# Retention and a mixture of experts in one kernel: the rows of zeros are written one per expert, and the fill branches are read by two engines alone

## The chip, the cores and the metric

One core of a Trainium2 chip runs the whole program. The metric is the device time of one execution in microseconds. The kernel before was timed in three runs: 432.47, 430.78 and 431.31 us, median 431.31. A separate execution was profiled; the rows and lines below come from it.

Engines: PE is TensorE (PEld its weight loads), DVE is VectorE, ACT is ScalarE, POOL is GpSimd, SP is SyncE, which issues most DMAs. POOL issues the indirect DMAs, those whose target rows are given by a list of indices.

## The reference

Two parts follow each other. The first is linear attention with a decay per head ("retention"); the second sends each of the 3072 tokens through the one of 8 experts that its gate likes best. Both in float32:

```python
# q, k, v: (4, 8, 768, 64)
for t in range(S):
    state = gamma[None, :, None, None] * state + np.einsum('bhd,bhe->bhde', k[:, :, t], v[:, :, t])
    y[:, :, t] = scale * np.einsum('bhd,bhde->bhe', q[:, :, t], state)
x = y.transpose(0, 2, 1, 3).reshape(3072, 512)

e_idx = np.argmax(x @ w_gate, axis=1)            # gate_w: softmax probability of e_idx
eom = 1.0 / (1.0 + np.exp(-(x @ w_output_gate)))
for e in range(8):
    mask = e_idx == e
    h = np.maximum(x[mask] @ w1[e], 0.0)         # (n, 512) @ (512, 1024)
    out[mask] = gate_w[mask, None] * eom[mask, e, None] * (h @ w2[e])
```

## The kernel before

**Attention loop.** The tokens are taken in 12 pairs of 128-row chunks. Pass j of the loop `for j in range(1, NPR - 1)` (L714 to L769) does the scores of pair j (`w`, L356), the output from the state (`py <- qt, sd`, L373) and from the scores (`py <- am, vs`, L380), and for pair j-1 the gate's logits, the choice of the expert, a place in the expert's stretch, and an indirect DMA that scatters the token's row to that place in a DRAM buffer `srt` (`scatter`, L532). `srt` has 448 slots for each expert. The instructions of every engine run in the order in which the code is written.

**Rows that stay empty.** An expert gets fewer than 448 tokens, so the slots behind its count hold nothing of this execution. They must say "no token" before they are read. `pad` (L186) writes rows of zeros to the slots from 320 on that are behind the count (indices of filled slots are out of bounds and skipped). If an expert has so few tokens that slots below 320 are empty too, `fill` (L543) does the rest, in branches: once for the first expert (L734, on the number `late`), and once for all (L831 and L835, on `n_low`). Such a branch needs the number in a register of each engine, which `nc.values_load` reads (TENSOR_LOAD), and a compare-and-branch.

**Experts.** The expert that leads after the first passes is taken first, in two halves: 224 rows are loaded in the attention loop (`head_load`, L580) and computed between the last attention passes (`head_all`, generator steps pulled by `run_head`), the rest is "expert 0" of the main loop. Then the seven others follow in the order of their counts. The main loop (L1042 on) has steps s, eight (f = 0 to 7) for each expert e: `stage1(s)` is h = x w1 for 128 columns (L899, 12 matmuls) with a relu on ACT and a low part on DVE, `stage2(s - 2)` adds to the output (L917, 12 matmuls). Every operand is split into a high and a low part, so three matmuls stand for one. At f = 1 SP issues the load of the next expert's rows (`load_x`, L848), which DVE and ACT turn and split in the steps that follow (L876, L877, L883). The output rows of expert e - 1 are sent on POOL, two DMAs a step (`emit`); those of the first half, seven, one a step while e = 0 (`emit_head`, L1072).

**Where the zeros are written.** `new_pad` (L975) issues the next `pad` on POOL behind a given instruction. Three are written in the code between the attention and the main loop (behind the relu of head steps 5, 6 and 7), the other four at steps 2 to 5 of the main loop behind that step's `stage2`. The tracker of dependencies sees one buffer `srt`, so each `new_pad` waits for earlier loads of `srt`, except those listed in `x0`, which holds the load of expert 0 alone.

Of the kernel before, what the change touches and what calls it, by code (L numbers as in the profile page):

```python
# [26 lines left out]
SEG = 130  # L27
ROW = 4 * SEG
NOID = float(1 << 20)


@with_exitstack
def retention_moe_kernel(
# [14 lines left out]
    nc = tc.nc  # L48
    P = 128
    B, H, S, D = q.shape  # L50
    E, DM, DF = w1.shape
# [7 lines left out]
    NF = DF // P  # L59
# [27 lines left out]
    n_low = cpool.tile([P, 2], I32, name="n_low")  # L87
    late = cpool.tile([P, 1], I32, name="late")
# [36 lines left out]
    def last_consts():  # L125
        nc.gpsimd.memset(zrow, 0.0)
        nc.gpsimd.memset(zrow.rearrange("p (a x) -> p a x", x=SEG)[:, :, P:P + 1], NOID)
        nc.gpsimd.memset(capk, float(SLOTS))
# [40 lines left out]
    def low_weights(s: int):  # L169
        subs.pop(s)()  # L170
# [31 lines left out]
    with tc.manual_schedule(engines=None), ExitStack() as actx:  # L202
# [27 lines left out]
        def load_pair(j):  # L230
            if j > 4:
                load_q(j)
                load2(vn, v, "vn", j, 2)
                load2(kn, k, "kn", j, 3)
            else:
                load2(kn, k, "kn", j, 3)
                load_q(j)
                load2(vn, v, "vn", j, 2)
# [55 lines left out]
        def prep_q(j, engine, after=()):  # L294
            qr[j] = ap.tile([P, 2, H, D], F32, name="qr", tag="qr", bufs=1)
            t = qn.pop(j)
            for r in range(2):
                o = engine.tensor_copy(qr[j][:, r], t[:, :, r])
                if r == 0:
                    behind(o, after)  # L300
# [242 lines left out]
        def fill(base, cnt, lo, hi, pool):  # L543

            for j in range(lo, hi, P):
# [6 lines left out]

                nc.vector.tensor_scalar(out=fi, in0=cnt, scalar1=sf, scalar2=NOID, op0=ALU.is_gt, op1=ALU.mult)
                ii = pool.tile([P, 1], I32, name="ii", tag="ii")
# [23 lines left out]
        hd = {}  # L578
# [93 lines left out]
        def read_pick():  # L672
            rank_e[0] = nc.values_load(pick[0:1, 0:1], engines=(mybir.EngineType.SP,), min_val=0, max_val=E - 1)
# [6 lines left out]
        def judge():  # L680
            first_count()
            nc.vector.tensor_scalar(out=late, in0=cnt0, scalar1=float(HEAD), scalar2=None, op0=ALU.is_lt)
            fi = sm.tile([P, 1], F32, name="fi0", tag="fi0")
            nc.vector.tensor_scalar(out=fi, in0=cnt0, scalar1=slot, scalar2=NOID, op0=ALU.is_gt, op1=ALU.mult)
            nc.vector.scalar_tensor_tensor(out=pad0, in0=slot, scalar=base0, in1=fi, op0=ALU.add, op1=ALU.add)
# [28 lines left out]
        for j in range(1, NPR - 1):  # L714
            if j + 2 < NPR:
                load_pair(j + 2)
            if j - 1 == PICK + 1:
                read_pick()
            if j in w_at:
                load_weights(w_at[j])  # L720
            if j - 2 == EARLY:
                scatter(j - 2, 0)
                scatter(j - 2, 1)
            prep_q(j + 1, nc.gpsimd, [rt["done"]] if j >= 2 else ())
            prep_v(j + 1, nc.gpsimd)
            if j >= 2 and j - 2 != EARLY:
                scatter(j - 2, 0)
            open_y()
            scores(j, (lambda: state(1, 0)) if j == 1 else None)
            if j - 1 in w_at:  # L730
                cast_weights(w_at[j - 1])
            inter(j)
            if j == EARLY + 2:
                n_late = nc.values_load(late[0:1, 0:1], min_val=0, max_val=1)  # L734
                with tc.If(n_late > 0):
                    fill(base0, cnt0, 0, HEAD, sm)
                head_load()
                load_weights(4)
            logits(j - 1)
            turn_k(j + 1)  # L740
            turn_l(j - 1)
            route1(j - 1)
            exps(j - 1)
            attend(j, 0)
            weigh(j, 0)
            if j % NJ < NJ - 1:
                state(j, 1)
            turn_q(j + 1)
            gates(j - 1)
            for c in {1: (3, 4), 2: (5,)}.get(j, ()):  # L750
                more_gq(c, nc.vector)
            if j - 1 in w_at:
                low_weights(w_at[j - 1])
            if j - 2 == PICK:
                choose()
            tokens(j - 1)
            labels(j - 1)
            rows(j - 1)
            counts(j - 1)
            if j >= 2 and j - 2 != EARLY:  # L760
                scatter(j - 2, 1)
            places(j - 1)
            if j - 1 == PICK:
                sort8(cnts, io8, pick)
            if j - 1 == EARLY:
                judge()
            attend(j, 1)
            weigh(j, 1)
            state(j + 1, 0)  # L769
# [58 lines left out]
        cast_weights(6)  # L828
        run_head(12)
        low_weights(6)  # L830
        n_few = nc.values_load(n_low[0:1, 0:1], min_val=0, max_val=E)  # L831
        with tc.If(n_few > 0):
            for e in range(E):
                fill(float(e * SLOTS), cnts[:, e:e + 1], FILL - P, FILL, sm)
            n_few = nc.values_load(n_low[0:1, 1:2], min_val=0, max_val=E)  # L835
            with tc.If(n_few > 0):
                for e in range(E):
                    fill(float(e * SLOTS), cnts[:, e:e + 1], 0, FILL - P, sm)

    with tc.manual_schedule(engines=None), ExitStack() as mctx:  # L840
# [7 lines left out]
        def load_x(e):  # L848
            r0, n = PASS[e]
            nb = math.ceil(n / 32)  # L850
            t = mp.tile([P, NB, SEG], F32, name="xl", tag="xl")
            for a in range(4):
                ld = nc.sync.dma_start(
                    t[32 * a:32 * a + 32, 0:nb],
                    srt[ds(r0, 32 * nb), a * SEG:(a + 1) * SEG].rearrange("(n i) x -> i n x", i=32))
                if e == 0:
                    behind(ld, sent)
                    x0.append(ld.ins)
                else:
                    behind(ld, pads[e:e + 1])  # L860
                    for o in pads[:e] + pads[e + 1:]:
                        tc.declare_no_dep(ld.ins, o, reason="other experts' rows")
            xr[e] = t

        def turn_x(e, dc):
# [101 lines left out]
        def prep_idl(m):  # L967
            t = mp.tile([P, NTB], I32, name="idl", tag="idl", bufs=1)
            nc.vector.tensor_scalar(out=t, in0=m, scalar1=0.25, scalar2=None, op0=ALU.mult)
            return t  # L970

        x0 = []
        pads = list(hd["pad"])

        def new_pad(after):  # L975
            r = len(pads)
            o = pad(padr[:, r - 1:r])
            behind(o, [after])
            for ld in x0:
                tc.declare_no_dep(o.ins, ld, reason="other experts' rows")  # L980
            pads.append(o.ins)

# [21 lines left out]
        fj = rpool.tile([P, E], F32, name="fj")  # L1004
        nc.vector.tensor_scalar(out=fj, in0=ck, scalar1=slot, scalar2=NOID, op0=ALU.is_gt, op1=ALU.mult)
        nc.vector.scalar_tensor_tensor(out=fj, in0=ordf, scalar=float(SLOTS), in1=fj, op0=ALU.mult, op1=ALU.add)
        nc.vector.tensor_scalar(out=padr, in0=fj, scalar1=slot, scalar2=None, op0=ALU.add)
        new_pad(hd["relu", 5])
        run_head(24)
        new_pad(hd["relu", 6])  # L1010
        run_head(12)
        turn_x(0, 0)
        turn_x(0, 1)
# [28 lines left out]
        for s in range(NS + 2):  # L1042
            e, f = divmod(s, NF)
            while loaded < min(NS, s + NF + 1):
                load_weights(loaded)
                loaded += 1
            if f == 1 and e + 1 < E:
                load_x(e + 1)
            if s == NS - NF:
                idm = load_idl(E - 1)  # L1050
            if s < NS:
                relu = stage1(s)
            if s >= 2:
                done = stage2(s - 2)
                if s - 2 < NF and len(pads) < E:
                    new_pad(done)
                if f == 1:
                    copy_out(s - 2)
            if e == 0:
                for n in SPLIT.get(f, ()):  # L1060
                    split_weights(n)
                for dc in {4: (0,), 5: (1,), 6: (2, 3)}.get(f, ()):
                    prep_x(1, dc)
            else:
                if 3 <= f < 7 and e + 1 < E:
                    prep_x(e + 1, f - 3)
                for n in SPLIT.get(s, (s + NF - 2,)):
                    if n < NS:
                        split_weights(n)
            if s == NS - NF + 3:  # L1070
                idl = prep_idl(idm)
            if e == 0:  # L1072
                if f < HEAD // 32:
                    behind(emit_head(f), [relu])
            elif s < NS and f >= 1:
                for n in range(2 * f - 2, min(math.ceil(PASS[e - 1][1] / 32), 2 * f)):
                    behind(emit(e - 1, n), [done if n % 2 else relu])
# [5 lines left out]
    with tc.If(odd > 0):  # L1083
        with ExitStack() as octx:
# [72 lines left out]
            for r in range(1, E):  # L1157
                nov = nc.values_load(over[0:1, r - 1:r], min_val=0, max_val=SLOTS)
                with tc.If(nov > 0):
                    e = nc.values_load(order[0:1, r - 1:r], engines=(mybir.EngineType.SP,), min_val=0, max_val=E - 1)  # L1160
# [47 lines left out]
```

## Time and profile before

| | |
|---|---|
| median of three runs | 431.31 us (430.78 to 432.47) |
| the profiled execution | 432.42 us |
| its span, first to last instruction | 430.7 us |
| mean granted TensorE clock | 0.99 |
| TensorE busy | 413.7 us, 96% |
| VectorE, ScalarE, GpSimd busy | 264.4, 179.3 and 190.2 us |
| bytes moved by DMA | 74.06 MB, mean 172 GB/s |

Busy time counts instructions of the engine itself; register, branch and semaphore instructions are not counted as busy. An idle time is put down to what ended it; "issue" means that the profile shows nothing that the engine waited for. The chain of waits is followed back from the last instruction. A DMA share is the mean busy share of 16 DMA engines.

### The profile page before, as it was taken

Reading aid. Unit: us, or ns where it says so; the run is one execution under the profiler, and the core shown is the slowest. Engines: PE = TensorE matmul, PEld = TensorE weight load, DVE = VectorE, ACT = ScalarE, POOL = GpSimd, SP = SyncE. Lnnn points to the kernel's source line nnn. Section 1 sums busy time; section 2 is a strip of 40 time slices with the busy share of each in tenths; the row PEclk is TensorE's granted clock in tenths of the full one; section 3 lists DMA queues with packets and bytes.
Section 4 is the critical chain, followed back from the end, with each engine's and each line's share of the span. In section 5 each row is a group of like instructions: output and inputs, shape, how many; then the busy total and the mean of one; then the engine's idle time right before and its main releaser. Section 6 shows DMA issues by size and latency. Waiting matters only on the chain.

```text
span 430.7 us, 10299 instructions
## 1 busy us (share of the span) xinstructions
PE 413.7 (96%) x3700; PEld 392.0 (91%) x3700; DVE 264.4 (61%) x703; ACT 179.3 (42%) x395; POOL 190.2 (44%) x257
## 2 busy tenths in 40 slices
PE   8999999999999998999999999999999999999990
PEld 4888999999879997899999999999999999999990
DVE  2888778778778765766466556655646656754120
ACT  2244565646436233635335334443434443542120
POOL 6558666676624217060045426405515524523512
PEclk9999999999999999999999999999999999999995
DMA  9999999995562398494475395485558458420102
GB/s 192 208 225 255 258 268 248 275 269 176 144 223 102 74 250 272 146 270 153 135 172 173 122 198 171 137 188 167 177 151 206 137 176 197 159 59 19 44 7 74
DMA packets 126566, 74.06 MB, mean 172 GB/s; under 512 B 56686, under 2 KB 114930, under 8 KB 126504
## 3 DMA queue, kind: packets, MB, share of 16 engines
q1 hardware_dynamic: 119568, 59.30, 55.1%
q0 software_dynamic: 5728, 13.93, 9.3%
q8 instruction: 31, 0.51, 0.5%
q14 instruction: 31, 0.25, 0.2%
q10 hardware_dynamic: 1208, 0.06, 0.2%
HBM read 59.35 MB, written 15.23 MB: 173 GB/s over the span
## 4 chain that ended last, share of the span: by engine, by line
PE 80%; issue 9%; DMA 3%; POOL 3%; DVE 2%; SPq 1%; ACT 1%; POOLq 0%; DVEq 0%; ACTq 0%
PE h L899 26%; PE a L917 26%; PE w L356 5%; PE py L380 5%; PE py L373 3%; POOL out_dram L177 3%; PE w L324 3%; PE w L342 2%; PE w L508 2%; PE st L396 2%; PE misc L407 2%; PE h L622 2%; DMA kn<-in_k_dram 1%; DMA srt<-row,posi 1%; PE w L643 1%
## 5 line engine op out<-in xcount | busy, mean ns | idle before, releaser
L177 POOL DMA_INDIRECT out_dram<-ot,idi x84 | 91.0, 1083 | 147.2 <-ACT whi L160 79.0
L899 PE MATMUL h<-xh,whi 128*128 128x224 f32 (+7 forms) x256 | 85.6, 334 | 1.1 <-issue 1.1
L899 PE MATMUL h<-xw,whi 128*128 128x224 f32 (+7 forms) x256 | 85.9, 335 | 0.6 <-issue 0.4
L899 PE MATMUL h<-xh,wlo 128*128 128x224 f32 (+7 forms) x256 | 85.4, 334 | 0.9 <-issue 0.9
L917 PE MATMUL a<-hh,whi 128*128 128x224 f32 (+7 forms) x256 | 85.8, 335 | 0.4 <-issue 0.3
L917 PE MATMUL a<-hl,whi 128*128 128x224 f32 (+7 forms) x256 | 85.8, 335 | 0.1
L917 PE MATMUL a<-hh,wlo 128*128 128x224 f32 (+7 forms) x256 | 85.7, 335 | 0.0
L904 DVE SCALAR_TENSOR_TENSOR hl<-h,hh 128x224 fp32r<-128x224 f32 (+7 forms) x64 | 35.0, 548 | 61.9 <-ACT hh L903 54.0
L903 ACT ACTIVATE hh<-h 128x224 fp32r<-128x224 f32 (+7 forms) x64 | 31.0, 484 | 82.1 <-PE h L899 74.7
L164 DVE TENSOR_TENSOR wlo<-raw,whi 128x512 fp32r<-128x512 f32 x64 | 43.9, 686 | 29.3 <-ACT whi L159 25.7
L159 ACT CAST whi<-raw 128x512 fp32r<-128x512 f32 x64 | 39.6, 619 | 37.7 <-PE a L917 33.4
L899 PEld LDWEIGHTS h<-xw,whi 128*128 128x128 f32 x256 | 48.2, 188 | 2.4 <-issue 1.3
L899 PEld LDWEIGHTS h<-xh,whi 128*128 128x128 f32 x256 | 48.2, 188 | 2.0 <-issue 1.6
L917 PEld LDWEIGHTS a<-hh,whi 128*128 128x128 f32 x256 | 48.2, 188 | 1.3 <-issue 0.9
L899 PEld LDWEIGHTS h<-xh,wlo 128*128 128x128 f32 x256 | 48.2, 188 | 0.9 <-issue 0.5
L917 PEld LDWEIGHTS a<-hl,whi 128*128 128x128 f32 x256 | 48.2, 188 | 0.6 <-DVE hl L904 0.2
L917 PEld LDWEIGHTS a<-hh,wlo 128*128 128x128 f32 x256 | 48.2, 188 | 0.4
L165 DVE TENSOR_TENSOR wlo<-raw,whi 128x512 fp32r<-128x512 f32 x64 | 43.8, 685 | 0.0
L160 ACT CAST whi<-raw 128x512 fp32r<-128x512 f32 x64 | 39.6, 618 | 0.1
L877 ACT CAST xh<-xt 128x416 fp32r<-128x416 f32 (+3 forms) x32 | 16.3, 513 | 40.4 <-DVE xt L876 29.8
L359 DVE TENSOR_TENSOR am<-w,mask 128x1024 f32<-128x1024 f32 x24 | 28.4, 1219 | 5.9 <-PE w L356 4.5
L532 POOL DMA_INDIRECT srt<-row,posi x24 | 24.7, 1030 | 11.0 <-issue 2.9
(183 smaller groups left out, 606.0 us busy)
## 6 DMA issues: line engine op xcount, KB each, us to landing
raw<-in_moe_w_dram SPq DMA_DIRECT2D x128, 256.0 KB
qn<-in_q_dram SPq DMA_DIRECT2D x12, 512.0 KB
kn<-in_k_dram SPq DMA_DIRECT2D x24, 256.0 KB
vn<-in_v_dram SPq DMA_DIRECT2D x24, 256.0 KB
xl<-srt SPq DMA_DIRECT2D x12, 211.2 KB
xl<-srt SPq DMA_DIRECT2D x12, 195.0 KB
out_dram<-ot,idi POOLq DMA_INDIRECT x84
xl<-srt SPq DMA_DIRECT2D x8, 113.8 KB
```

The lines of the kernel that those rows point to most:

```text
L159: nc.scalar.copy(hi[:, 0], raw[:, 0])
L160: nc.scalar.copy(perm(hi), r2)
L164: nc.vector.tensor_sub(lo[:, 0], raw[:, 0], hi[:, 0].bitcast(F32))
L165: nc.vector.tensor_sub(perm(lo), r2, perm(hi).bitcast(F32))
L177: st = nc.gpsimd.indirect_dma_start(out=dst, out_offset=bass.IndirectOffsetOnAxis(ap=idx, axis=0), in_=src, in_offset=None, bounds_check=n ...
L356: nc.tensor.matmul(w[:, hh, g * P:(g + 1) * P], kt[j][half[hh], c, g], qt[j][half[hh], g, c], start=True, stop=True)
L359: nc.vector.tensor_tensor(out=a.rearrange("p b g t -> p (b g) t"), in0=w.rearrange("p b (g t) -> p (b g) t", g=NG), in1=mask.rearrange("p ...
L532: st = nc.gpsimd.indirect_dma_start(out=srt, out_offset=bass.IndirectOffsetOnAxis(ap=posi[:, c:c + 1], axis=0), in_=row[:, c].rearrange("p ...
L899: nc.tensor.matmul(ps[:, 0:C], l[:, 0, w], r[:, dc, 0:C], start=(n == 0), stop=(n == 3 * NDC - 1))
L903: relu = nc.scalar.activation(hh, ps[:, 0:C], AF.Relu)
L904: nc.vector.scalar_tensor_tensor(out=hl, in0=ps[:, 0:C], scalar=0.0, in1=hh.bitcast(F32), op0=ALU.max, op1=ALU.subtract)
L917: mm = nc.tensor.matmul(accs[d][:, 0:C], l[:, 1, w], r, start=(f == 0 and n == 0), stop=(f == NF - 1 and n == 2))
```

## The change

Three things. The reads of `late` and `n_low` go to POOL and DVE alone (`FILLERS`), the two engines that do something in the branches. Of the seven `new_pad` calls, two stay between attention and main loop (behind the relu of head steps 5 and 7), and the other five are made at the first step of experts 1 to 5, behind that step's relu. And the list of loads for which a `new_pad` doesn't wait now has every load of expert rows (`xloads`).

```diff
--- before.py
+++ after.py
@@ -27,6 +27,7 @@
 SEG = 130
 ROW = 4 * SEG
 NOID = float(1 << 20)
+FILLERS = (mybir.EngineType.Pool, mybir.EngineType.DVE)
 
 
 @with_exitstack
@@ -731,7 +732,7 @@
                 cast_weights(w_at[j - 1])
             inter(j)
             if j == EARLY + 2:
-                n_late = nc.values_load(late[0:1, 0:1], min_val=0, max_val=1)
+                n_late = nc.values_load(late[0:1, 0:1], engines=FILLERS, min_val=0, max_val=1)
                 with tc.If(n_late > 0):
                     fill(base0, cnt0, 0, HEAD, sm)
                 head_load()
@@ -828,11 +829,11 @@
         cast_weights(6)
         run_head(12)
         low_weights(6)
-        n_few = nc.values_load(n_low[0:1, 0:1], min_val=0, max_val=E)
+        n_few = nc.values_load(n_low[0:1, 0:1], engines=FILLERS, min_val=0, max_val=E)
         with tc.If(n_few > 0):
             for e in range(E):
                 fill(float(e * SLOTS), cnts[:, e:e + 1], FILL - P, FILL, sm)
-            n_few = nc.values_load(n_low[0:1, 1:2], min_val=0, max_val=E)
+            n_few = nc.values_load(n_low[0:1, 1:2], engines=FILLERS, min_val=0, max_val=E)
             with tc.If(n_few > 0):
                 for e in range(E):
                     fill(float(e * SLOTS), cnts[:, e:e + 1], 0, FILL - P, sm)
@@ -855,11 +856,11 @@
                     srt[ds(r0, 32 * nb), a * SEG:(a + 1) * SEG].rearrange("(n i) x -> i n x", i=32))
                 if e == 0:
                     behind(ld, sent)
-                    x0.append(ld.ins)
                 else:
                     behind(ld, pads[e:e + 1])
                     for o in pads[:e] + pads[e + 1:]:
                         tc.declare_no_dep(ld.ins, o, reason="other experts' rows")
+                xloads.append(ld.ins)
             xr[e] = t
 
         def turn_x(e, dc):
@@ -969,14 +970,14 @@
             nc.vector.tensor_scalar(out=t, in0=m, scalar1=0.25, scalar2=None, op0=ALU.mult)
             return t
 
-        x0 = []
+        xloads = []
         pads = list(hd["pad"])
 
         def new_pad(after):
             r = len(pads)
             o = pad(padr[:, r - 1:r])
             behind(o, [after])
-            for ld in x0:
+            for ld in xloads:
                 tc.declare_no_dep(o.ins, ld, reason="other experts' rows")
             pads.append(o.ins)
 
@@ -1007,7 +1008,6 @@
         nc.vector.tensor_scalar(out=padr, in0=fj, scalar1=slot, scalar2=None, op0=ALU.add)
         new_pad(hd["relu", 5])
         run_head(24)
-        new_pad(hd["relu", 6])
         run_head(12)
         turn_x(0, 0)
         turn_x(0, 1)
@@ -1052,8 +1052,6 @@
                 relu = stage1(s)
             if s >= 2:
                 done = stage2(s - 2)
-                if s - 2 < NF and len(pads) < E:
-                    new_pad(done)
                 if f == 1:
                     copy_out(s - 2)
             if e == 0:
@@ -1069,6 +1067,8 @@
                         split_weights(n)
             if s == NS - NF + 3:
                 idl = prep_idl(idm)
+            if e > 0 and f == 0 and len(pads) < E:
+                new_pad(relu)
             if e == 0:
                 if f < HEAD // 32:
                     behind(emit_head(f), [relu])
```

On PE, in pass 10 of the attention loop: `py` are the matmuls from the state, `misc` those of the logits that follow. Before:

```order
L373 MATMUL py<-qt,sd 64x128 [waits DVE_49,Activation_49]
L373 MATMUL py<-qt,sd 64x128 x13
L734 TENSOR_LOAD late [waits DVE_49]
L735 COMPARE_AND_BRANCH
L735 UNCONDITIONAL_BRANCH x2
L407 MATMUL misc<-yt,wg 32x128 x8
```

and after:

```order
L374 MATMUL py<-qt,sd 64x128 [waits DVE_49,Activation_49]
L374 MATMUL py<-qt,sd 64x128 x9
L736 UNCONDITIONAL_BRANCH
L374 MATMUL py<-qt,sd 64x128 x4
L408 MATMUL misc<-yt,wg 32x128 x8
```

The load and the compare are gone, and one jump, which stands four matmuls earlier, stays. At the second place, L831, it is the same.

On POOL, from the end of the second branch on: `padr` are the writes of zeros, `out_dram<-ot_...,idx_...` the seven output DMAs of the first half, `out_dram<-ot,idi` those of expert 0. Before:

```order
L187 DMA srt<-zrow,padr 6784x520 [waits DMAHW1_49,DMAHW2_49,DMASW3_49,DMAHW3_49,DMASW2_49,DMAHW4_49,DVE_49,Activation_49]
L187 DMA srt<-zrow,padr 6784x520 [waits DMASW4_49,Activation_49]
L187 DMA srt<-zrow,padr 6784x520 [waits DMASW5_49,Activation_49]
L177 DMA out_dram<-ot_3288,idx_2438 12288x128 [waits DMASW6_49,DVE_49,Activation_49]
L177 DMA out_dram<-ot_3288,idx_2438 12288x128 [waits DMASW7_49,Activation_49]
L187 DMA srt<-zrow,padr 6784x520 [waits DMAHW5_49,DMAHW6_49,DMAHW0_49,DMAHW7_49,DMASW0_49,PE_49]
L177 DMA out_dram<-ot_3288,idx_2438 12288x128 [waits DMASW1_49,Activation_49]
L187 DMA srt<-zrow,padr 6784x520 [waits PE_49]
L177 DMA out_dram<-ot_3288,idx_2438 12288x128 [waits DMASW3_49,Activation_49]
L187 DMA srt<-zrow,padr 6784x520 [waits DMASW4_49,PE_49]
L177 DMA out_dram<-ot_3288,idx_2438 12288x128 [waits DMASW5_49,Activation_49]
L187 DMA srt<-zrow,padr 6784x520 [waits DMASW6_49,PE_49]
```

and after:

```order
L188 DMA srt<-zrow,padr 6784x520 [waits DMAHW1_49,DMAHW2_49,DMASW3_49,DMAHW3_49,DMASW2_49,DMAHW4_49,DVE_49,Activation_49]
L188 DMA srt<-zrow,padr 6784x520 [waits DMASW4_49,Activation_49]
L178 DMA out_dram<-ot_3276,idx_2435 12288x128 [waits DMASW5_49,DVE_49,Activation_49]
L178 DMA out_dram<-ot_3276,idx_2435 12288x128 [waits DMASW6_49,Activation_49]
L178 DMA out_dram<-ot_3276,idx_2435 12288x128 [waits DMASW7_49,Activation_49]
L178 DMA out_dram<-ot_3276,idx_2435 12288x128 [waits DMASW0_49,Activation_49]
L178 DMA out_dram<-ot_3276,idx_2435 12288x128 [waits DMASW1_49,Activation_49]
L178 DMA out_dram<-ot_3276,idx_2435 12288x128 [waits Activation_49]
L178 DMA out_dram<-ot_3276,idx_2435 12288x128 [waits DMASW3_49,Activation_49]
L188 DMA srt<-zrow,padr 6784x520 [waits DMASW4_49,Activation_49]
L178 DMA out_dram<-ot,idi 12288x128 [waits DMAHW5_49,DMAHW6_49,DMASW5_49,DMAHW7_49,DVE_49,Activation_49]
```

The seven output DMAs now follow each other without writes of zeros between them; the fourth write, which waited for four DMA semaphores (the load of expert 1) and for PE, is now the third, stands behind them and waits for ACT.

## Rows read from the trace of the kernel before

**Rows 1.** The page's head and busy times of the engines: us, share of span, instructions.
```profile
span 430.7 us, 10299 instructions
...
PE 413.7 (96%) x3700; PEld 392.0 (91%) x3700; DVE 264.4 (61%) x703; ACT 179.3 (42%) x395; POOL 190.2 (44%) x257
```

**Rows 2.** Chain of waits: start, length in us; scores of passes 7, 8, 10, 11.
```profile
76.81 1.99 PE w L356 x32
...
86.47 1.99 PE w L356 x32
...
105.39 1.99 PE w L356 x32
...
116.50 1.99 PE w L356 x32
```

**Rows 3.** Timeline, TensorE in pass 10: start, length, and in brackets idle before.
```profile
108.69 0.45 PE L373 MATMUL py<-qt,sd 64*64 64x128 f32 x5 [0.30 <-issue]
109.44 0.42 PE L373 MATMUL py<-qt,sd 64*64 64x128 f32 x2 [0.30 <-issue]
```

**Rows 4.** Chain of waits, where the second expert begins.
```profile
166.98 1.34 PE a L917 x12
...
176.07 2.37 PE h L899 x12
178.44 1.33 PE a L917 x12
```

**Rows 5.** Source line 734, the read of late: duration ns, start.
```profile
L734 SPq FUSED_REGOPS  x1: 160/160/160, 106.5 to 106.5; - x1
...
L734 SPq SEQ_ASSERT  x1: 18/18/18, 106.7 to 106.7; - x1
...
L734 PEldq TENSOR_LOAD <-late x1: 486/486/486, 108.7 to 108.7; - x1
```

**Rows 6.** Source line 735, the branch, on PE.
```profile
L735 PEldq COMPARE_BRANCH  x1: 228/228/228, 109.3 to 109.3; - x1
```

**Rows 7.** Source line 831, the read of n_low, on PE.
```profile
L831 PEldq TENSOR_LOAD <-n_low x1: 312/312/312, 137.9 to 137.9; - x1
```

**Rows 8.** Three stretches: busy us, instructions, clock, DMA share, GB/s.
```profile
136.00:140.00 4.00, 4.00 (x38) 4.00 (x37) 3.23 (x12) 2.78 (x6) 1.28 (x2) 1.00 0.35 135
156.00:160.00 4.00, 4.00 (x38) 4.00 (x37) 2.78 (x6) 1.94 (x5) 0.00 (x0) 1.00 1.19 223
184.00:188.00 4.00, 4.00 (x22) 3.77 (x21) 2.12 (x5) 1.68 (x3) 3.08 (x4) 1.00 1.13 206
```

**Rows 9.** Waits of SP's queue: us in total, times, longest.
```profile
SPq L584 <- DMA srt<-row,posi: 5.4, 1, 5.4
...
SPq L853 <- DMA srt<-row,posi: 3.2, 1, 3.2
```

**Rows 10.** Timeline, POOL's indirect DMAs.
```profile
144.86 0.98 POOL L187 DMA_INDIRECT srt<-zrow,padr  x1 [7.27 <-ACT h L627]
...
161.98 0.98 POOL L187 DMA_INDIRECT srt<-zrow,padr  x1 [7.67 <-PE h L899]
...
172.35 0.98 POOL L177 DMA_INDIRECT out_dram<-ot,idx  x1 [0.30 <-issue]
183.75 1.27 POOL L177 DMA_INDIRECT out_dram<-ot,idi  x1 [10.42 <-issue]
```

**Rows 11.** Timeline, VectorE on the second expert's input.
```profile
161.15 0.18 DVE L872 CAST idi<-xl 128x14 int32<-128x14 f32 x1 [1.38 <-DMA xl<-srt]
...
169.80 0.63 DVE L883 TENSOR_TENSOR xw<-xt,xh 128x448 fp32r<-128x448 f32 x1 [0.63 <-issue]
```

**Rows 12.** Timeline, SP's load of the second expert's rows.
```profile
151.75 2.31 SPq L853 DMA_DIRECT2D xl<-srt  x4
```

**Rows 13.** Timeline, ScalarE's relu of step 4.
```profile
158.98 0.36 ACT L903 ACTIVATE hh<-h 128x224 fp32r<-128x224 f32 x1 [0.31 <-PE h L899]
```

**Rows 14.** Timeline, TensorE in the slow stretch.
```profile
169.10 0.36 PE L899 MATMUL h<-xh,whi 128*128 128x436 f32 x1 [0.79 <-issue]
...
174.81 0.37 PE L917 MATMUL a<-hh,whi 128*128 128x224 f32 x1 [0.33 <-issue]
```

## The prediction

> **What bounds the kernel now.** I read the head of the page and its table of busy times first. The profiled execution took 432.42 us for a span of 430.70, so 1.72 us lie around the span; the median of the three runs, 431.31, is 1.11 below it. TensorE is busy 413.7 of 430.7 us [rows 1]. With only 17 us of gaps, a change that adds and removes no matmul can win only what lies in gaps of TensorE, so the next view is the chain of waits, read for places where a repeated pattern takes longer than its neighbours. The reader is to see two.
>
> The first is in the attention loop. A pass of the loop runs from one `w L356` to the next. Pass 7, 76.81 to 86.47, takes 9.66 us; pass 10, 105.39 to 116.50, takes 11.11 [rows 2]. Both have j % 3 = 1, so they issue the same attention matmuls. The excess is 1.45 us, and pass 10 is the one that holds the first read of `late`. The timeline of TensorE shows where: the `py` matmuls come in pieces, with gaps called "issue" [rows 3].
>
> The second is where the second expert begins. The matmuls of one stage-2 step ended at 166.98 + 1.34 = 168.32; the h step of 12 matmuls and the a step behind it were over at 176.07. That is 7.75 us, where the next such pair takes 2.37 + 1.33 = 3.70 [rows 4]. So 4.05 us are lost there. After 176 the chain runs from matmul group to matmul group, so what is won here or earlier should reach the end.
>
> **The reads and branches taken from PE, ACT and SP.** Removed on each of the three: two register loads and two compare-branches on the path that is run. What stays is one unconditional jump at each place, because DVE and POOL still need the If as a block of its own.
>
> At the first place PE's load takes 0.49 us from 108.7 [rows 5], and its compare starts at 109.3 and takes 0.23 [rows 6], so the pair ends at 109.54, 0.8 us after it began. The other 0.65 of the 1.45 lie ahead of the load, and no row says what they are. Bounds of the gain: nothing, if the excess belongs to something else in this pass, and 1.45, if all of it is the read. No other view shows an unconditional jump with its time; I let the one that stays cost as much as the compare, 0.23, and take 1.45 - 0.23 = 1.2 us, near the upper end, because no other pass shows the excess.
>
> [...]
>
> At the second place (n_low) PE's load takes 0.31 us [rows 7], but PE is busy 4.00 of 4.00 us in the stretch around it [rows 8]: the matmuls already queued, 0.11 us apart, cover it. Gain 0; without that cover it would be some 0.5. ACT waits for PE at both places, so its loads cost nothing. SP is released from the reads, but at both places it then waits 5.4 and 3.2 us for scattered rows to land [rows 9], and those landings do not move: 0. Two register operations that guard the value (0.16 + 0.02 us, [rows 5]) move from SP to POOL at each place, 0.36 us in all; POOL idles 7.27 us before its next work at the second [rows 10] and is busy 44% of the span [rows 1]: 0.
>
> **The rows of zeros.** Seven indirect DMAs write them, before and after, at 0.98 us each on POOL. Before, three go out from 144.86, and the fourth is held until 161.98, when the load of the second expert's rows has landed: the row names PE as the releaser, but the write's list of waits has the four DMA semaphores of that load too, and DVE gets the rows 0.83 us earlier [rows 10, 11]. The output rows of the first half-expert stand behind it in POOL's queue. POOL then issues nine indirect DMAs in a row, until 172.35 + 0.98 = 173.33. After, two go out at the start, the seven output DMAs follow their own relu, and the other five writes of zeros come one per expert. None needs TensorE: their price on the path is 0. One more POOL DMA per expert costs 1.3 us with its issue, on an engine that is idle more than half the time. Nor can a later write of zeros hold a load: each is now issued a whole expert, eight step pairs of 3.70 us or some 30 us, before the load that needs it.
>
> What moves is traffic. The load for the second expert is issued at 151.75 [rows 12] and DVE gets its rows at 161.15 [rows 11]. Two output DMAs went out inside that time; now it is five, since relu number 4 (from 0) is at 158.98 [rows 13]. Three more DMAs of 128 x 512 B are 197 KB. At the 223 GB/s of 156 to 160 [rows 8] that is 0.9 us; at best nothing. One write of zeros at 147 goes. In the kernel as it is PE would not see 0.9 us, since it is slow then anyway.
>
> **The slow stretch at 168 to 175.** It is the term that I cannot size. DVE has the last piece of the second expert's input at 169.80 + 0.63 = 170.43 [rows 11]. At full speed h would have started at 168.32 and wanted that piece at about 170.3, so data explain 0.3 us at most of the 4.05; 3.7 are gaps called "issue" [rows 14]. They lie under POOL's burst, which starts 6.3 us ahead of them and ends 1.5 us before PE is back at its pace. That speaks for a link. Against it: from 183.75 on [rows 10] POOL issues indirect DMAs again, with the DMA engines at a share of 1.13 [rows 8], and PE keeps its pace. Bounds for the change: 0 and 3.7. I take 0 for the likeliest case, because nothing in the trace names POOL as the releaser.
>
> **Sum.** 1.2 + 0 + 0 + 0 = 1.2 us. Against the profiled execution 432.42 - 1.2 = 431.2; against the median 431.3 - 1.2 = 430.1. That is 0.28%, under the 0.5% (2.2 us) that a measurement of this kernel can tell from no change.
>
> **The rivals.**
> - The slow stretch goes with POOL's burst. For: it is the only large gap left, it lies under the burst, and the change takes seven of the nine DMAs out of it. Against: the later bursts without effect. 3.7, less up to 0.9 for the later input, is 2.8 to 3.7, say 3.2; with the 1.2 that is 4.4: 426.9 us.
> - The change doesn't do what it says for PE: the jump that stays costs what the load did, and the slow stretch stays too. For: 0.65 us of the excess come ahead of the load. 431.3 us.
> - Slower: the output DMAs delay the second expert's input. Five of them, 328 KB, at half of the 206 GB/s that a stretch with both queues busy shows [rows 8] are 3.2 us, so DVE would have the last piece at 173.6 and the pair of steps would be over at 173.6 + 0.4 + 1.33 = 175.3, no later than the 176.07 of today. It decides only if the slow stretch is tied to the work and not to the hour, so that its 4.05 us come behind that wait: 179.4, which is 3.3 later, less the 0.8 that the read's own span gives: 2.5 slower, 433.8 us. For: the DMA share is above 1 there already. Against: two output DMAs inside the same stretch did no visible harm.
>
> **How the numbers follow.** Forecast (430.1) 0.40; doesn't do what it says (431.3) 0.12; slow stretch goes (426.9) 0.37; slower (433.8) 0.11. Faster by over 0.5%: the 0.37, and 0.02 for a forecast case that also wins a part of the stretch, 0.39. Slower: 0.11. Within: 0.50. The range that leaves out the slower case and the lowest part of the faster one is 426.3 to 432.8; the forecast's own, with the read worth between 0 and 1.45 and the runs' own spread, is 429.3 to 431.9.
>
> **What will show it.** Right: pass 10 as long as pass 7 within 0.3 us; the seven output DMAs of the first half-expert spread from 152 to 168; five writes of zeros one per expert, each early in it; PE's pace unchanged after 176. Wrong: pass 10 still over 11 us (the read was not its cause); the pair of steps at the second expert's start down to some 4 us (rival one) or over 9 with DVE waiting for the rows past 163 (the slower case).

## The result and the profile after

The changed kernel takes 427.25 us, median of four runs (426.36 to 428.27), against 431.7 us for the kernel before in four runs (430.78 to 432.47). The ratio is 0.9895, with a 95% interval of 0.986 to 0.9929: faster by 1.05%. The time lies inside the range given, but the likeliest case said 430.1 and was 2.85 us too high; what happened is close to the first rival, for which 426.9 was worked out. The two traces were taken at a mean granted clock of 0.990 and 0.992; over 60 runs of the kernel before, taken beside the experiments (one slow run left out), it goes from 0.984 to 0.994, and the 15 runs at 0.986 or below took 433.4 us on average, the 20 at 0.992 or above 430.1.

The page of the changed kernel, its head and busy times; they answer to [rows 1].

```profile
span 426.6 us, 10284 instructions
...
PE 413.0 (97%) x3700; PEld 392.6 (92%) x3700; DVE 263.5 (62%) x703; ACT 179.2 (42%) x395; POOL 190.2 (45%) x257
```

The span is 4.1 us shorter and TensorE's work the same, so gaps went. Lines are left out at each `...`. The chain of waits (start, length, engine, line) of the changed kernel, at the places of [rows 2] and [rows 4]:

```profile
105.38 1.99 PE w L357 x32
...
116.35 1.99 PE w L357 x32
```

```profile
167.02 1.34 PE a L918 x12
168.36 1.97 PE h L900 x10
170.32 0.03 issue
170.35 0.67 PE h L900 x2
171.02 1.34 PE a L918 x12
172.36 2.37 PE h L900 x12
```

Pass 10 of the attention loop takes 10.97 us instead of 11.11: 0.14 won where 1.2 was forecast. The 0.14 do not even reach the end, since the steps ahead of the second expert end at 168.36, 0.04 later than before. The pair of steps there takes 4.00 us instead of 7.75, and ends 3.71 us earlier (172.36 against 176.07). So almost the whole gain of 4.1 us is the slow stretch at 168 to 175.

TensorE's timeline in pass 10 of the changed kernel, against [rows 3]: the two gaps called "issue" are there still, with no read and no compare left on TensorE.

```profile
107.30 1.08 PE L374 MATMUL py<-qt,sd 64*64 64x128 f32 x27
108.70 0.44 PE L374 MATMUL py<-qt,sd 64*64 64x128 f32 x4 [0.32 <-issue]
109.44 0.27 PE L374 MATMUL py<-qt,sd 64*64 64x128 f32 x1 [0.29 <-issue]
```

GpSimd's indirect DMAs of the changed kernel, against [rows 10]: the burst of nine from 161.98 is dissolved.

```profile
162.64 0.99 POOL L178 DMA_INDIRECT out_dram<-ot,idx  x1 [2.00 <-ACT hh L904]
166.24 0.98 POOL L178 DMA_INDIRECT out_dram<-ot,idx  x1 [2.61 <-ACT hh L904]
172.67 1.19 POOL L188 DMA_INDIRECT srt<-zrow,padr  x1 [5.45 <-DVE wlo L165]
178.44 1.26 POOL L178 DMA_INDIRECT out_dram<-ot,idi  x1 [4.58 <-issue]
```

VectorE on the second expert's input, against [rows 11]:

```profile
160.78 0.17 DVE L873 CAST idi<-xl 128x14 int32<-128x14 f32 x1 [0.70 <-issue]
...
169.67 0.63 DVE L884 TENSOR_TENSOR xw<-xt,xh 128x448 fp32r<-128x448 f32 x1 [0.63 <-ACT xh L878]
```

It starts 0.37 us earlier than before, although five outputs were issued inside the load's time (from 152.08 to 159.64): they did not delay it.

### The profile page after: what moved, and what is told of

It reads as the page before. It is cut to its first block, busy times and chain, and to the rows that moved or that the text cites. A ratio compares the mean times of both kernels' runs of the same rounds, so it can differ in the third digit from the quotient of the medians.

```text
span 426.6 us, 10284 instructions
## 1 busy us (share of the span) xinstructions
PE 413.0 (97%) x3700; PEld 392.6 (92%) x3700; DVE 263.5 (62%) x703; ACT 179.2 (42%) x395; POOL 190.2 (45%) x257
## 4 chain that ended last, share of the span: by engine, by line
PE 85%; issue 8%; POOL 3%; DVE 1%; ACTq 1%; ACT 0%; POOLq 0%
PE h L900 26%; PE a L918 26%; PE py L381 6%; PE w L357 6%; PE py L374 3%; PE w L343 3%; PE w L325 3%; POOL out_dram L178 3%; PE h L623 3%; PE w L509 2%; PE st L397 2%; PE misc L408 2%; PE w L644 2%; PE w L312 1%; ACTq L878 1%
```

## The experiments

Two questions were open. Which part of the change removes the slow stretch, and why does pass 10 keep its excess? Theory A puts the stretch down to TensorE's reads and branches, theory B to GpSimd's burst. A and B are told apart by one half of the change at a time.

**fillers_only**, the edit of the reads alone:

```diff
-                n_late = nc.values_load(late[0:1, 0:1], min_val=0, max_val=1)
+                n_late = nc.values_load(late[0:1, 0:1], engines=FILLERS, min_val=0, max_val=1)
```

and the same at the two reads of `n_low`.

> The kernel before with the reads of late and n_low on GpSimd and VectorE alone; the rows of zeros stay as before, so the burst of nine indirect DMAs from 162 to 173 us on GpSimd stays. Theory A (the slow stretch comes from what TensorE reads and branches on, or from where its instructions then lie): the stretch at 168 to 175 goes, the pair of steps takes about 4.0 us instead of 7.75, and the time is 427.3 to 427.6. Theory B (the stretch comes from GpSimd's burst): the pair stays at 7.75, only the 0.14 us of pass 10 is won, 431.5. Both: pass 10 takes 10.97 us.

Measured: 431.49 us, ratio to before 0.9984 (0.9955 to 1.0012), no difference that can be told. Chain of waits of this kernel:

```profile
167.65 1.66 PE h L900 x8
...
175.36 3.38 PE h L900 x12
```

The pair takes 7.71 us. Pass 10 takes 11.00.

**pads_only**, the writes of zeros alone (`xloads`, two at the start, one at each of experts 1 to 5).

> The kernel before with the writes of zeros moved (two at the start, one each at experts 1 to 5, no waits on other experts' loads); late and n_low are still read by all engines. Theory B (GpSimd's burst): the pair of steps at the second expert's start takes about 4.0 us and the time is 427.4 to 427.7. Theory A (TensorE's reads and branches): the pair stays at about 7.75 us and the time at 431.7.

Measured: 428.36 us, ratio 0.9908 (0.9871 to 0.9944), the whole gain of the change within the interval. The pair takes 4.32 us (168.63 to 172.95). TensorE's waits from 150 to 300 us (what for: us, times, longest) hold no gap called "issue" any more:

```profile
PE h L899 <- DVE xw L883: 0.2, 1, 0.2
```

Theory A falls, B stands.

**no_branch1** and **no_branch2** leave out one branch of the kernel before each, with its reads and fills.

> The kernel before without the first branch (read of late, compare, fill and jump left out; the rows that it would fill need no filling with this input). Tells what the first branch costs TensorE in all, jump included. If the whole excess of pass 10 is the branch: pass 10 takes 9.7 us instead of 11.11 and 1.4 us are won there. If the excess belongs to something else in this pass: 11.1. Theory B leaves the slow stretch where it is (sum 430.3); theory A lets the stretch change as well, since TensorE's instructions after it stand elsewhere (sum 426.5 if it goes).

Measured: 430.74 us, ratio 0.9998 (0.9973 to 1.0023). Pass 10 takes 10.76 us (105.11 to 115.87), so 0.35 of the 1.45 go with the branch. One gap stays, where no branch stands any more. TensorE's timeline:

```profile
108.41 0.43 PE L373 MATMUL py<-qt,sd 64*64 64x128 f32 x3 [0.29 <-issue]
```

The slow stretch stays without the first branch too: between 150 and 300 us TensorE's gaps called "issue" come to 2.4 us, against 2.7 in the kernel before.

> The kernel before without the second branch (both reads of n_low, compares, fills and jumps left out; no row needs this filling with this input). Theory A: the slow stretch some 30 us behind that branch goes, 427.6. Theory B: it stays, 431.7. Pass 10 stays at 11.11 us in both.

Measured: 429.52 us, ratio 0.997 (0.9938 to 1.0003), between the two times expected, so that the time alone tells nothing. The trace does. GpSimd's timeline at the burst's start and TensorE's chain of waits at the first gap:

```profile
159.22 0.98 POOL L187 DMA_INDIRECT srt<-zrow,padr  x1 [6.26 <-PE a L908]
```

```profile
165.74 0.60 issue
```

The burst starts 2.76 us earlier than in the kernel before, and TensorE's gaps begin 6.5 us behind the burst's start, where it was 6.3 in the kernel before (168.32). The stretch stays without the branch, and follows the burst.

What in the burst does it? Theory C: the number of indirect DMAs that GpSimd issues one right behind the other. Theory D: the data that wait in its queue.

**xloads_only**: the only edit is that each load of rows is listed, so the writes of zeros keep their places in the code but wait for nothing.

> The kernel before, where only the list of loads for which a write of zeros doesn't wait is extended: the four writes of zeros at steps 2 to 5 go out behind their step (2.7 us apart, an output between two of them) instead of in a burst from 162 us. Theory C (the burst: TensorE stalls from about the sixth of the indirect DMAs that GpSimd issues one right behind the other): no burst, no stall, the pair of steps at the second expert's start takes 4.0 to 4.3 us, time 427.4 to 428. Theory D (data: 876 KB of zeros and outputs that wait in GpSimd's queue, whatever the issue's pace): 330 KB per 2.7 us go beside the loads, which alone move 220 GB/s, so the queue fills up all the same; a stall of some us between 160 and 172, time 430 to 432.

Measured: 427.73 us, ratio 0.9878 (0.9856 to 0.9899). Between 155 and 169 us there are nine issues as in the burst, but with a pause of 0.5 to 0.8 us behind most pairs of them. TensorE's waits from 150 to 300 us name data, not "issue":

```profile
PE h L899 <- ACT xh L877: 0.5, 1, 0.5
PE h L899 <- DVE xw L883: 0.4, 2, 0.2
```

The pair takes 5.60 us (168.28 to 173.88), not the 4.0 to 4.3 expected: the last pieces of input come later here. The time is against theory D, which wanted 430 to 432.

**burst_empty**, in the changed kernel (shortened; `nopad` holds indices that are all out of bounds):

```diff
-                if f < HEAD // 32:
-                    behind(emit_head(f), [relu])
+                if f == 5:
+                    for n in range(HEAD // 32):
+                        if n < 4:
+                            behind(pad(nopad[:, n:n + 1]), [relu])
+                        behind(emit_head(n), [relu])
```

> The changed kernel, but the seven outputs of the first half-expert are held to step 5 (about 162 us) and go out in one burst, with four added writes of zeros between them whose indices are all out of bounds, so that they move nothing. Eleven indirect DMAs in a row from 162 to 175, but 459 KB instead of the burst's 1240 KB before. Theory C (number of issues one behind the other): TensorE stalls from the sixth, 168.5, the pair of steps takes 6.5 to 8 us, time 430 to 432. Theory D (data waiting): no stall, pair 4.0 us, time 427.2 to 427.8.

Measured: 434.74 us, ratio 1.005 (1.0022 to 1.0078). The stall is back, though GpSimd's queue moves 0.45 MB (162 to 179 us) where it moved 1.04 in the kernel before (162 to 176). TensorE's waits from 150 to 300 us:

```profile
PE a L919 <- issue: 1.6, 2, 0.8
PE h L901 <- issue: 1.5, 4, 0.7
```

Its gaps run from 171.6 to 178 us, beside a row of eleven issues from 162.33 to 176.79; they begin at the eighth (171.56), not at the sixth. The time is above the 430 to 432 expected: at the stall's end and behind it the granted clock is 0.50 (176 to 180 us); eight matmuls from 178.11 take 3.05 us, where twelve from 182.50 take 2.37. D falls.

**pads_burst**: the changed kernel with `while` for `if` at the `new_pad` of expert 1, so that five writes of zeros go out in a row.

> The changed kernel, but the five writes of zeros that go out one per expert all go out one behind the other at the first step of expert 1, from 172.7 us on: five times up to 266 KB. Theory C (number): the seven outputs of expert 0 come next from 178.4, so there are up to twelve in a row, and a stall from the sixth, about 179, of 3 us or more; 430 to 431. Theory D (data): a stall from the third or fourth, 176 on, 430 to 432. If it was neither but the moment (what TensorE runs or fetches at 168): no stall, 427.3.

Measured: 426.81 us, ratio 0.9868 (0.9846 to 0.989). Eleven issues in a row, from 172.12 to 188.17 (the second took 2.62 us) and 1.15 MB on GpSimd's queue, and no stall; TensorE's waits from 150 to 300 us:

```profile
PE h L900 <- DVE xw L884: 0.2, 1, 0.2
```

So a count alone is not the rule, or the moment matters. That was asked next.

**two_bursts**: rows of empty writes at two other places of the changed kernel (shortened).

```diff
+            for n in range({(0, 0): 8, (2, 3): 9}.get((e, f), 0)):
+                o = pad(nopad[:, n % E:n % E + 1])
+                behind(o, [relu])
```

> The changed kernel with two bursts of added writes of zeros, all indices out of bounds, so that they move nothing: eight behind the relu of the main loop's first step (151.5 to 162, where TensorE's matmuls have 224 columns and start 0.11 us apart; five outputs follow at once), and nine behind a relu of the third expert (matmuls of some 420 columns, 0.2 us apart). Theory C1 (any long row of issues stalls TensorE): a stall some 6 to 9 us into each, from 158 to 161 on and again in the later one, 3 us or more each; 433 to 436. Theory C2 (only while TensorE takes instructions at the faster pace): a stall in the first alone, 430 to 433. Theory C3 (only at one place of TensorE's instructions, the stretch that ran at 168 to 176 in all kernels so far): the first burst stalls it only from 168 on, the later one not; 428 to 431.

Measured: 447.47 us, ratio 1.0371 (1.0322 to 1.042), slower than any theory had it. Both rows stall TensorE (C1). GpSimd's first row and TensorE's timeline beside it:

```profile
150.49 0.98 POOL L189 DMA_INDIRECT srt<-zrow,nopad  x1 [3.81 <-ACT hh L907]
...
156.94 0.99 POOL L189 DMA_INDIRECT srt<-zrow,nopad  x1 [0.30 <-issue]
```

```profile
157.59 0.27 PE L903 MATMUL h<-xh,whi 128*128 128x224 f32 x1 [0.83 <-issue]
158.29 0.26 PE L903 MATMUL h<-xw,whi 128*128 128x224 f32 x1 [0.44 <-issue]
159.02 0.37 PE L903 MATMUL h<-xh,wlo 128*128 128x224 f32 x1 [0.46 <-issue]
```

The sixth issue starts at 156.94, and from there TensorE begins one matmul, or a few, about every 0.7 us instead of every 0.11. The second row (17 issues with the outputs around it, 225.66 to 247.94) has gaps of up to 1.4 us from 242 to 250, so they begin only at its thirteenth issue (241.59). The clock adds to the loss: busy time by engine, granted clock (third from the right), DMA share and GB/s, for a stretch at the first stall's end and one behind each of the two:

```profile
164.00:166.00 2.00, 0.78 (x3) 1.07 (x4) 0.00 (x0) 0.00 (x0) 0.53 (x1) 0.50 0.87 285
170.00:172.00 2.00, 2.00 (x11) 2.00 (x11) 1.01 (x3) 0.92 (x3) 0.29 (x1) 0.50 0.76 262
250.00:252.00 2.00, 2.00 (x6) 1.91 (x6) 1.11 (x2) 0.70 (x2) 0.98 (x1) 0.50 0.11 40
```

At 170 TensorE is busy all the time again, but at a granted clock of 0.50.

**rows_of_issues**: the same edit with two, four, six, eight and ten empty writes at the fourth step of experts 2 to 6.

> The changed kernel with added writes of zeros whose indices are all out of bounds (they move nothing), behind the fourth step's relu of experts 2, 3, 4, 5 and 6: two, four, six, eight and ten of them. With the outputs in front of and behind them the rows of issues without a pause of 0.4 us or more are about 4, 7, 10, 13 and 17 long. Theory C (TensorE stalls from about the sixth issue of a row): no stall at expert 2, 0 to 2 us at expert 3, and then some 1.2 us more for each issue more: 3 to 6, 6 to 10, 10 to 15 us. If only the number of all indirect DMAs in a stretch counts, or their data: no stall, or the same small one at all five. If the stall, once it is there, lasts as long as a fixed time and not as long as the row: 3 to 7 us at each of the last three.

Measured in a single run: 452.22 us, beside one of 432.36 for the kernel before. Rows of issues with pauses under 0.45 us, by GpSimd's timeline, and what TensorE waited for "issue" beside them:

| expert | row, us | issues | TensorE's waits |
|---|---|---|---|
| 2 | 215.18 to 227.24 | 9 | none |
| 3 | 251.34 to 265.91 | 11 | none |
| 4 | 286.90 to 305.62 | 14 | 1.4 us |
| 5 | 323.85 to 343.16 | 15 | 4.4 us |
| 6 | 364.97 to 389.06 | 18 | 5.0 us |

The last of these, TensorE's waits from 360 to 405 us:

```profile
PE h L903 <- issue: 4.5, 7, 1.5
PE a L921 <- issue: 0.5, 2, 0.3
```

The direction is that of theory C, the count is not: the rows came out longer than I had reckoned, and 9 and 11 in a row passed without a stall where 9 stalled the kernel before. Wherever a row stalls TensorE, its last gap ends 0.8 to 2 us after the row's last issue.

Laid beside the pace of TensorE, the rows of all these kernels agree better than by their count. Where a matmul starts every 0.11 us, the first gap comes 6.3 to 6.6 us into the row (the kernel before, no_branch1, no_branch2, the first row of two_bursts). Where the pace goes from 0.11 to 0.20 us on the way, it comes 7.7 to 9.3 us into it (spaced_before, fillers_only, burst_empty). Where one starts every 0.17 us, it comes after 12.6 and 14.9 us (experts 5 and 6 above), and at 0.18 to 0.19 after 17.8 (expert 4) and 16.6 (the second row of two_bursts). The rows that passed, at 0.19 to 0.20 us, were over before that: after 12.1 and 14.6 us (experts 2 and 3) and 16.1 (pads_burst). This was read from the traces afterwards; no run varies the pace alone, so it is a pattern and not shown to be the cause.

One more rival, that TensorE waits there for its instructions to be fetched, can be laid beside the DMA queues. In the kernel before, from 160 to 165 us, from 165 to 170 and from 170 to 175 (packets, MB, share of 16 engines):

```profile
q8 instruction: 1, 0.02, 1.6%
...
q1 hardware_dynamic: 970, 0.83, 50.0%
q0 software_dynamic: 296, 0.61, 31.3%
...
q0 software_dynamic: 184, 0.43, 23.5%
q1 hardware_dynamic: 1, 0.00, 0.0%
```

The queues named "instruction" move nothing from 165 to 175 us, while the gaps run, so this rival has nothing for it in the trace.

**spaced_scatter** asks for the same cause in pass 10, where two scatters follow each other in the changed kernel:

```profile
106.60 0.99 POOL L533 DMA_INDIRECT srt<-row,posi  x1 [0.63 <-DVE pad L686]
107.89 0.98 POOL L533 DMA_INDIRECT srt<-row,posi  x1 [0.30 <-issue]
```

The changed kernel, with

```diff
                 scatter(j - 2, 0)
-                scatter(j - 2, 1)
             prep_q(j + 1, nc.gpsimd, [rt["done"]] if j >= 2 else ())
             prep_v(j + 1, nc.gpsimd)
+            if j - 2 == EARLY:
+                scatter(j - 2, 1)
```

> The changed kernel, but in pass 10 of the attention loop the second of the two scatters that GpSimd issues one behind the other at 106.6 and 107.9 us comes behind GpSimd's two next pieces of work, at about 111. If the gap of TensorE at 108.4 (ahead of the jump, and there too when the branch is left out) is tied to GpSimd's third indirect DMA in a row: it goes, and pass 10 takes 10.2 to 10.4 us instead of 10.97. If it belongs to something else: 10.97. In both cases the first half-expert's rows land 3 us later than 112.9, which may cost up to 3 us later on: 426.5 to 430.

Measured: 425.82 us, ratio 0.9837 (0.9817 to 0.9858), better than expected. GpSimd's scatters and TensorE's timeline:

```profile
106.58 0.98 POOL L533 DMA_INDIRECT srt<-row,posi  x1 [0.63 <-DVE pad L686]
110.76 1.02 POOL L533 DMA_INDIRECT srt<-row,posi  x1 [0.17 <-POOLq L737]
```

```profile
107.28 1.12 PE L374 MATMUL py<-qt,sd 64*64 64x128 f32 x32
108.33 0.64 PE L408 MATMUL misc<-yt,wg 128*32 128x128 f32 x16
```

No gap is left in the pass, and it takes 9.67 us (105.37 to 115.04), as pass 7. The jump is still there. The span is 2.5 us shorter than the changed kernel's (424.1 against 426.6), of which the pass gives 1.30 and the first pair of the second expert 0.30 (3.70 against 4.00); the rest was not followed up.

**spaced_before**, the same edit in the kernel before, prices the read.

> The kernel before, in which only the second scatter of pass 10 comes behind GpSimd's next two pieces of work (about 111 us instead of 107.9); late and n_low are still read by all five engines, and the burst at 162 stays. It prices the read, compare and jump on TensorE where GpSimd issues no indirect DMA next to them. Theory R (the read itself holds TensorE): pass 10 takes 10.4 to 10.5 us (9.66 + 0.8), against 9.67 with the read on GpSimd and VectorE alone. Theory S (the whole excess of 1.45 us belongs to the scatter issued right behind another): 9.7 us. The stretch at 168 to 175 stays in both; time 430.3 (S) or 431 (R).

Measured: 431.05 us, ratio 0.9996 (0.9973 to 1.0019). Pass 10 takes 10.49 us (104.89 to 115.38): theory R. The read and the gap that it leaves with the compare:

```profile
L735 PEldq TENSOR_LOAD <-late x1: 769/769/769, 107.5 to 107.5; - x1
```

```profile
108.67 0.64 PE L407 MATMUL misc<-yt,wg 128*32 128x128 f32 x16 [0.70 <-issue]
```

In this run the stall of the burst was followed by a granted clock of 0.50, which the profiled run of the kernel before had not shown. First a stretch of the kernel before, then two of this run:

```profile
174.00:176.00 2.00, 1.67 (x14) 1.45 (x13) 0.58 (x2) 1.08 (x3) 0.00 (x0) 1.00 0.03 8
...
172.00:174.00 2.00, 1.41 (x7) 1.41 (x7) 1.26 (x3) 1.77 (x4) 0.09 (x1) 0.51 0.10 33
174.00:176.00 2.00, 2.00 (x7) 1.86 (x7) 2.00 (x4) 2.00 (x5) 0.00 (x0) 0.50 0.18 49
```

The 0.6 us won in pass 10 do not show in the time; the interval is about 1 us wide to either side.

**spaced_both** adds to spaced_scatter a later second scatter in the last pass (`scatter(j - 2, 1, [attend(j, 0)])`).

> The changed kernel, with the two scatters of pass 10 apart and those of the last pass apart too (the second behind the first half's attention matmuls, 121 us instead of 117.5). If the gap of TensorE at 118.4 us (0.5 to 1.2 us in all kernels so far) is tied to the second of two scatters, it goes, and the time is 0.4 to 1.0 below that of the kernel with pass 10 alone mended: 424.8 to 425.5. If it is not, 425.8, and the gap stays or moves by less than 0.5 us.

Measured: 425.6 us, ratio 0.9868 (0.9833 to 0.9904). The gap at 118 is gone; from pass 10's start to the second h step of the first half it is 19.04 us instead of 19.89. In the span nothing is left of it (424.0 against 424.1), and the times are not told apart. Both beat the changed kernel's own median, by 1.4 and 1.65 us, in other runs than its own.

## Why the prediction was right or wrong

- **The sum of the likeliest case was wrong**, though the direction and the range held: 1.2 us were forecast, 4.45 measured between the medians. That the time came out within 0.4 us of the first rival's 426.9 is in part luck: the rival added 3.2 for the stretch and 1.2 for the reads, and the traces show 3.71 and 0.14.
- **The reads on TensorE** is the step that failed: "1.45 - 0.23 = 1.2 us, near the upper end, because no other pass shows the excess". Two causes lay over each other in pass 10, and only one of them was the change's. With the scatters apart, the read and its compare cost 0.82 us (10.49 against 9.67). With the read gone, the scatters one behind the other cost 1.30 (10.97 against 9.67). Together they cost 1.45, less than their sum, so taking away one of them wins little: 0.14 here, 0.35 without the branch. From run to run that varies: with adjacent scatters the pass took 11.01 to 11.88 in four kernels that read on all engines, and 10.74 to 11.00 in six that read on two; by the means (11.46 and 10.90) the read is worth 0.56. All these are single traced executions. The row that named the other cause, GpSimd's scatter at 107.89, stood in that engine's timeline of the kernel before; I did not lay it beside the gaps.
- **The jump** was put at 0.23, as much as the compare. It costs nothing that shows: in spaced_scatter it stands in pass 10, and the pass takes 9.67 us, as long as pass 7 with 9.66. So the unexplained 0.65 us were not the jump.
- **n_low, ACT and SP at 0** held: fillers_only gains nothing that can be told.
- **The rows of zeros at 0** failed in one point, the slow stretch: "I take 0 for the likeliest case, because nothing in the trace names POOL as the releaser". No view names a releaser for this stall; "issue", which means that the profile shows nothing that TensorE waited for, is all that stands there. The position under the burst was the better evidence. Rival one priced it at 2.8 to 3.7; 3.71 was won.
- **The later burst without effect**, my ground against rival one, was no counterexample of weight: from 183.75 GpSimd issues too, but it is a row of six, 7.7 us long, with a matmul every 0.2 us; at about that pace rows of 9 and 11 passed without a stall in rows_of_issues.
- **The slower case** did not occur: VectorE had the rows at 160.78, before the 161.15 of [rows 11].

What stays open: by what way an issue on GpSimd holds up TensorE, and what sets when it begins. The number of issues, their data and the place in TensorE's program were each varied, and none alone decides. A row's length and TensorE's pace taken together fit every row seen here, but no run tests them by themselves.

## What to carry to other kernels

A gap called "issue" on TensorE is worth laying beside the timelines of all the other engines before it is put down to TensorE's own instructions: here a row of indirect DMAs on GpSimd lay over those that cost most, at 168 to 175 us. Spread indirect DMAs out, with other work or a wait between them: that won 3.71 us at the second expert's start and 1.30 in pass 10, with GpSimd busy only 44% and 45% of the span. The DMAs need not move anything: the rows of two_bursts, with eight and nine empty writes, took the ratio from 0.9895 to 1.0371. And where two causes may lie over the same gap, take each away with the other gone; one at a time shows neither.

## What was not expected of the hardware

An indirect DMA that moves nothing takes GpSimd the same 0.98 us (two_bursts, 150.49) as one that writes rows ([rows 10]), and a row of eight of them with three outputs behind holds up TensorE as well. Some stalls of TensorE cost twice: behind them the granted clock stands at 0.50 for 4 to 6 us with TensorE busy 1.85 to 2.00 of each 2.00 us, as in two_bursts (250 to 254 and 166 to 172) and spaced_before (174 to 178); that fits the spread of the kernel before's times, given with the result. The read of a register took TensorE 0.31, 0.49 and 0.77 us at the places and runs shown, and its compare 0.23 us, where VectorE's and GpSimd's compares in the changed kernel took 0.07 and 0.05.
